# Attention with beacon keys and a maxout FFN on one core: batch 0's products by whole parts, a load gate one pair later, FFN two units ahead, no bank reordering

## The chip, the core and the metric

The kernel runs on one core of a Trainium2 chip. The metric is the device time of one execution in microseconds (us). TensorE (PE) multiplies matrices into PSUM (eight banks of 512 float32 columns on 128 partitions); VectorE (DVE), ScalarE (ACT) and GpSimd (POOL) do the rest; SyncE (SP) and GpSimd issue the transfers. Each engine works through its own instructions in the order in which they are written; semaphores hold an instruction until what it needs is there.

## The reference, cut to what matters

B = 8 batches, H = 8 heads, S = 576 tokens of D = 64, Nb = 16 beacon keys ahead of the tokens, d_model = 512, d_ff = 768.

```python
k_all, v_all = [beacon_k, k], [beacon_v, v]        # 592 keys
scores = q @ k_all.T / 8, causal over the 576 tokens, beacons always seen
a = exp(scores - max) / sum
x = (a @ v_all) as [4608 tokens, 512]
h = max(x @ w1, x @ w2, x @ w3)                    # [4608, 768]
out = h @ w_out                                    # float32
```

## The kernel before, in words

**Attention.** Heads go in pairs: pair p is two heads of batch p // 4, and two pairs make a quad (half of a batch). Scores are made transposed, keys on the partitions in five tiles t = 0..4 (128 keys each, the last 80), queries on the free axis; because of the mask, tile t needs only queries from 112, 240, 368 and 496 on. `emit_burst` (line 532) makes the scores of a pair (line 521, 12 matmuls) in four groups; each group takes a pair of PSUM banks, so a burst goes through all eight, in the order that `next_pairs` gives: bank pairs that were used longest ago first. ScalarE takes the exponential of each group (L541, L515 in batch 0), GpSimd (in batch 0 VectorE) masks it. `emit_pv_whole` (line 656) then makes a quad's sums over the keys (a product with ones, part 0) and its value products (parts 1 and 2: the even and the odd channels of four heads), line 684. ScalarE copies the products out (L694, L695) and inverts the sums by logarithm and exponential; `finish` (line 708) multiplies the two on VectorE into xT (L711), the transposed activations in a ring of four batches. The FFN of a block reads xT.

**Batch 0** is written by hand in `first_batch` (line 937), with scores of single pairs between other work, and with `pv_rest` (line 610) for the products of queries from 64 on: EARLY spans end at query 288 (HALF), LATE spans go from there to 576. P(quad, parts, early tiles, late tiles) emits some of them, line 592. `multiply_rest` (L648) multiplies products straight out of PSUM into xT; `invert_rest` makes the inverse sums on ScalarE (L633, L634). Early and late columns of one part lie in one bank.

**FFN.** It is cut into units, 22 for each block of 512 tokens: 18 first products (line 733; for each of six slices of d_ff the three weights i = 0, 1, 2), then four output products (line 786). i = 0 is copied into hT (L752), i = 1 and 2 are joined by a maximum on VectorE (L750); outputs are copied to y (L793) and stored by SP. In the first block the units are ordered and halved otherwise (line 763). A matmul of 512 columns takes a slot of 0.22 us, a first product four slots, an output product six. Units need xT of all their tokens. From pair 8 on, `emit_all` (line 1092) emits for each pair: the burst, every second pair the products of the quad before, then as many units as `allowed` admits (line 1107), then `finish`. The last unit of each step is the closing one: it is cut into 352 and 160 columns (CLOSE) in the two banks of the pair that `last_pair` gives, and drained in two halves. For a copy, ScalarE takes the 352 and VectorE the 160; for a maximum, VectorE takes both. The first unit is followed by the next pair's transposes (L405, up to pair 15), the second by the planned casts and loads. After pair 31 come its products, four units, `finish` and the rest of the units.

**Loads.** Batches 0 and 1 of q and k come through GpSimd's queue, cast on the way (`load_cast`, line 253), as do the FFN weights (`load_w`, L343; `load_w_out`, L346). The rest come through SP into seven staging buffers (L226, L305) and GpSimd casts them (L276, L321). The first of these for batch 2 are held back by a small memset on GpSimd (the gate, L224), emitted in `second_batch` (line 1046) among pair 6's masks. In that function pairs 4 to 7 run with three units each; `late_banks` moves two banks of quad 2's products to the end of the list of free banks, ahead of pair 8's burst.

Of the kernel before, what the change touches and what calls it, by code (L numbers as in the profile page):

```python
# [17 lines left out]
def kernel(  # L18
# [13 lines left out]
    nc = tc.nc  # L32

    B, H, S, D = q.shape
# [16 lines left out]
    HALF = S // 2  # L51


    n_kt = (NK + 127) // 128
# [3 lines left out]
    q_min = [max(0, t0) for t0 in k_tok]  # L58
# [545 lines left out]
            out = bank[:, part * HEAD : (part + 1) * HEAD]  # L604
            pv_matmuls(quad, part, out, 0, 0, HEAD, True, True)

    EARLY = [(0, HEAD, HALF), (1, q_min[1], HALF), (2, q_min[2], HALF)]
    LATE = [(t, max(HALF, q_min[t]), S) for t in range(n_kt)]

    def pv_rest(quad, parts, early, late=()):  # L610
        for part in parts:
            bank = pv_tiles[quad][part]
            for spans, ts in ((EARLY, early), (LATE, late)):
                for t in ts:
                    _, q0, q1 = spans[t]
                    pv_matmuls(
                        quad,
                        part,
                        bank[:, q0 - HEAD : q1 - HEAD],
                        t,  # L620
                        q0,
                        q1,
                        t == 0,
                        t == len(spans) - 1,
                    )

    def invert_heads(quad):
        nc.vector.reciprocal(recips[quad][:, 0:HEAD], pv_tiles[quad][3][:, 0:HEAD])
# [22 lines left out]
            recips[quad][:, None, q0:q1].to_broadcast([128, i1 - i0, q1 - q0]),  # L651
        )

    late_banks = []

    def emit_pv_whole(quad, order=(0, 1, 2, 3), split=False):
        b, g = divmod(quad, n_quad)
        v_sb = v_tiles[b]
        for p in range(PPQ * quad, PPQ * (quad + 1)):
            assert all((p, gi) in masked for gi in range(NG))  # L660
        banks = [next_bank() for _ in range(4)]
        banks = [banks[i] for i in order]
        late_banks[:] = [banks[0], banks[3]]
        every = range(n_kt)
        early = every[: V_PIECES[1][0]] if split else every
        runs = [(0, banks[0], 0, HEAD, S, every)]
        runs += [(part, banks[part], 0, HEAD, S, early) for part in (1, 2)]
        runs += [(part, banks[3], part * HEAD, 0, HEAD, every) for part in range(3)]
        if split:
            runs += [(part, banks[part], 0, HEAD, S, every[len(early) :]) for part in (1, 2)]  # L670
        for part, bank, lo, qa, qb, some in runs:
            ts = [t for t in every if q_min[t] < qb]
            for t in ts:
                if t not in some:
                    continue
                q0 = max(qa, q_min[t])
                n = k_rows[t]
                for j in range(4):
                    lhsT = (
                        ones[0:n]  # L680
                        if part == 0
                        else v_sb[0:n, t, head(g, j), part - 1 : D : 2]
                    )
                    nc.tensor.matmul(  # L684
                        acc[32 * j : 32 * j + 32, bank, lo + q0 - qa : lo + qb - qa],
                        lhsT,
                        at_view(PPQ * quad + j // 2, t, j % 2, q0, qb),
                        start=(t == 0),
                        stop=(t == ts[-1]),
                        tile_position=(0, 32 * j),  # L690
                    )
        raw = pv_pool.tile([128, 2, S], FP32, name="raw")
        for part in (1, 2):
            nc.scalar.copy(raw[:, part - 1, HEAD:S], acc[:, banks[part]])  # L694
        nc.scalar.copy(  # L695
            raw[:, :, 0:HEAD],
            acc[:, banks[3], HEAD : 3 * HEAD].rearrange("p (i c) -> p i c", i=2),
        )
        recip = nrm_pool.tile([128, S], FP32, name="recip")
        nc.scalar.activation(out=recip[:, HEAD:S], in_=acc[:, banks[0]], func=AF.Ln)  # L700
        nc.scalar.activation(out=recip[:, 0:HEAD], in_=acc[:, banks[3], 0:HEAD], func=AF.Ln)
        exp = partial(nc.scalar.activation, out=recip, in_=recip, func=AF.Exp, scale=-1.0)
        if split:
            between_exps.append(exp)
        else:
            exp()

        def finish():
            c0 = b % RING * S
            for i in range(2):  # L710
                nc.vector.tensor_mul(xT[:, 2 * g + i, c0 : c0 + S], raw[:, i], recip)  # L711
            if g == n_quad - 1:
                ready[0] = 2 * b + 1

        return finish
# [164 lines left out]
    def next_load(n=1, **gate):  # L880
        for _ in range(n):
            if loads:
                loads.pop(0)(**gate)
# [53 lines left out]
    def first_batch():  # L937
        T(2, 0, 0, 6, by_act)
        T(3, 0, 0, 7)
        load_v(0, 0, nc.vector)  # L940
        load_v(0, 1)
        load_beacons(1, B_PE, bk32_1)
        S_(1, 0)
        T(2, 0, 1, 5)
        T(3, 0, 1, 4)
        S_(2, 0)
        T(0, 1, 0, 6)
        T(0, 1, 1, 7)
        S_(3, 0)
        T(1, 1, 0, 5)  # L950
        T(1, 1, 1, 4)
        M(0, 0, True)
        S_(0, 1)
        fill(6)
        S_(0, 2)
        T(2, 1, 0, 6)
        T(3, 1, 0, 4)
        M(1, 0, True)
        S_(1, 1)
        T(2, 1, 1, 7)  # L960
        T(3, 1, 1, 5)
        S_(1, 2)
        S_(0, 3)
        for p in range(PPB):
            M(p, 1)
        M(0, 2, True)
        M(1, 2, True)
        V(0)
        load_w(0, [0])
        V(1)  # L970
        load_w(0, [1])
        V(2)
        load_cast(PPB)
        load_w(1, [0])
        V(3)
        load_w(1, [1])
        V(4)
        load_cast(PPB + 1)
        load_cast(PPB + 2)
        load_w(2)  # L980
        load_cast(PPB + 3)
        open_pv(0, acc[:, 4], acc[:, 5:7], acc[:, 7])
        P(0, (0,), (0, 1, 2))
        pv_heads(0)
        S_(1, 3)
        M(0, 3, True)
        M(1, 3, True)
        S_(2, 1)
        P(0, (0,), (), (0, 1, 3))
        S_(2, 2)  # L990
        M(2, 0, True)
        M(3, 0, True)
        P(0, (0,), (), (2, 4))
        S_(3, 1)
        M(2, 2, True)
        invert_heads(0)
        multiply_heads(0)
        P(0, (1, 2), (0, 1))
        S_(3, 2)
        S_(2, 3)  # L1000
        M(3, 2, True)
        P(0, (1, 2), (2,), (0, 1))
        S_(3, 3)
        M(2, 3, True)
        M(3, 3, True)
        P(0, (1, 2), (), (2,))
        first = sc_psum.tile()
        open_pv(1, first[:, 0], sc_psum.tile(), first[:, 1])
        P(1, (0,), (0, 1, 2))
        pv_heads(1)  # L1010
        P(1, (0,), (), (0, 1, 3))
        P(1, (0,), (), (2, 4))
        P(1, (1, 2), (0, 1, 2))
        for quad in range(n_quad):
            invert_rest(quad, HEAD, HALF)
        invert_heads(1)
        multiply_rest(0, HEAD, HALF)
        multiply_heads(1)
        for i in range(2):
            multiply_rest(1, HEAD, HALF, i, i + 1)  # L1020
        P(1, (1, 2), (), (0, 1, 2))
        for quad in range(n_quad):
            P(quad, (1, 2), (), (3,))
        for quad in range(n_quad):
            P(quad, (1, 2), (), (4,))
        ready[0] = 0
        for quad in range(n_quad):
            invert_rest(quad, HALF, S)
            multiply_rest(quad, HALF, S)
        by_act(bk16_1, bk32_1)  # L1030
        ready[0] = 1
        F_in(7, by_act)
        F_in(3, by_dve)
        F_in(4, by_act)
        turn_beacons(1, B_PE, bk16_1)
        place_beacons(PPB, by_act)
        F_in(5, by_dve)
        F_in(6, by_act)
        free_banks[:] = [0, 1, 2, 7, 3, 4, 5, 6]
        turn_pair(PPB, by_act)  # L1040
        load_v(1, 0, nc.vector)
        load_v(1, 1)
        drain[0] = by_dve
        F(1, last_pair(), True)

    def second_batch():
        for p in range(PPB, 2 * PPB):
# [6 lines left out]
            for gi in range(NG):  # L1054
                emit_masks(p, gi)
                if p == PPB + 2 and gi == 1:
                    cast_v(1, 0, by_pool)
            if p == PPB + 2:
                next_load(gate=nc.gpsimd)
                next_load(4)  # L1060
                cast_v(1, 1, by_pool)
            if p + 1 < 2 * PPB:
                F(1, next_psum)
# [5 lines left out]
        finish = emit_pv_whole(n_quad, (2, 0, 1, 3), True)  # L1069
        F(1, next_psum)  # L1070
        F(1, last_pair(), True)
        for i in late_banks:
            free_banks.remove(i)
            free_banks.append(i)
        return finish

    for p in range(B_PE * PPB, NPAIR):
# [14 lines left out]
    def emit_all():  # L1092
# [6 lines left out]
        for p in range(2 * PPB, NPAIR):  # L1099
# [4 lines left out]
            finish = emit_pv_whole(p // 2 - 1) if p % 2 == 0 else None  # L1104
            for gi in range(NG):
                emit_masks(p, gi)
            allowed = max((b - 1) * UPB + (-2, 4, 10, 16)[pi], done[0] + 2)
            n = 0
            while may_emit(allowed):
                n_y = len(y_out)  # L1110
# [60 lines left out]
```

## Time and profile before

| | |
|---|---|
| median of three runs | 284.36 us (284.12 to 284.95) |
| the profiled execution's own time | 284.03 us |
| its span, first to last instruction | 282.2 us |
| granted TensorE clock | 0.999 |
| busy: PE, DVE, ACT, POOL | 271.6, 171.1, 162.8, 133.0 us |
| mean busy share of the DMA engines until 230 us | about 0.9 and over |
| moved by DMA | 48.82 MB |

Times in the views count from the first instruction. A line of a timeline gives start, length, engine, line of the kernel, operation, what is written and read, the shape of the first of the merged instructions, how many, and in brackets the idle time ahead and what ended it. TensorE's lengths include the way through the array, so that neighbours overlap; starts are exact, and differences of starts are what the text uses. A few matmuls are missing from the counts. "issue" is time in which an engine waited for nothing that the profile shows.

### The profile page before, as it was taken

The page shows a single profiled execution, that of the slowest core. Times are in us where ns is not written, and L with a number is a line of the kernel's source. Part 1 is how long each engine was busy: PE and PEld are TensorE (multiplying, and loading weights), DVE is VectorE, ACT ScalarE, POOL GpSimd, SP SyncE. Part 2 cuts the span into 40 slices and gives each one's busy share as a digit, 9 for nine tenths or more (in the row PEclk, how much of TensorE's full clock was granted, in tenths as well). Part 3 has the DMA queues.
Part 4 walks back from the last instruction along what each step waited for, and adds up shares of the span by engine and source line. Part 5 has one row for each costly group of instructions (what it writes and reads, how often), then busy time and mean ns, then how long its engine had stood idle before and what let it go on. Part 6 is the DMA issues. An engine that isn't in the chain of part 4 may idle for free.

```text
span 282.2 us, 7689 instructions
## 1 busy us (share of the span) xinstructions
PE 271.6 (96%) x3020; PEld 156.4 (55%) x3050; DVE 171.1 (61%) x307; ACT 162.8 (58%) x307; POOL 133.0 (47%) x273
## 2 busy tenths in 40 slices
PE   7788999999999999999999999999999999999994
PEld 3557765556555555555556886555555554444442
DVE  4885655574837566464737382638363847876872
ACT  4995797978668566756675758585857540000000
POOL 7194378557286946475557655683245300000000
PEclk9999999999999999999999999999999999999999
DMA  8999989989997999999999999979745003003004
GB/s 145 214 180 204 219 159 159 241 200 293 275 205 229 199 241 245 186 249 207 250 194 189 252 243 242 187 161 236 184 105 172 0 2 149 2 1 149 0 0 149
DMA packets 85315, 48.82 MB, mean 173 GB/s; under 512 B 64416, under 2 KB 80032, under 8 KB 85280
## 3 DMA queue, kind: packets, MB, share of 16 engines
q1 hardware_dynamic: 78320, 42.25, 66.7%
q0 software_dynamic: 6544, 5.80, 13.5%
q8 instruction: 23, 0.38, 0.6%
q10 hardware_dynamic: 416, 0.30, 0.4%
q14 instruction: 12, 0.10, 0.1%
HBM read 35.13 MB, written 14.22 MB: 175 GB/s over the span
## 4 chain that ended last, share of the span: by engine, by line
PE 92%; ACT 4%; DVE 2%; issue 1%; DVEq 0%
PE acc L733 46%; PE acc L786 16%; PE acc L684 11%; PE acc L521 8%; PE acc L763 4%; ACT at_sb L515 4%; PE acc L405 2%; PE acc L465 1%; PE acc L592 1%; PE acc L804 0%; PE acc L506 0%; PE acc L424 0%; DVE kT L432 0%; DVE hT L750 0%; DVE busy L184 0%
## 5 line engine op out<-in xcount | busy, mean ns | idle before, releaser
L733 PE MATMUL acc<-xT,w_sb 128*128 128x512 bf16 (+4 forms) x728 | 134.2, 335 | 1.5 <-issue 0.2
L750 DVE TENSOR_TENSOR hT<-hT,acc 128x512 bf16<-128x512 bf16 (+1 forms) x104 | 70.2, 677 | 62.5 <-PE acc L733 55.2
L733 PEld LDWEIGHTS <-w_sb 128*128 128x128 bf16 x752 | 69.8, 98 | 59.5
L565 POOL TENSOR_SCALAR_AFFINE_SELECT at_sb<-at_sb 128x256 bf16<-128x256 bf16 x168 | 61.1, 385 | 81.5 <-ACT at_sb L541 80.8
L541 ACT ACTIVATE at_sb<-acc 128x208 bf16<-128x208 f32 (+3 forms) x140 | 89.6, 735 | 5.2 <-PE acc L521 3.3
L786 PE MATMUL acc<-w_out_sb,hT 128*128 128x512 bf16 (+2 forms) x241 | 48.3, 348 | 0.3
L752 ACT CAST hT<-acc 128x352 bf16<-128x352 f32 x18 | 8.1, 452 | 46.9 <-PE acc L733 46.9
L276 POOL CAST p<-st 96x768 bf16<-96x768 f32 x44 | 35.0, 824 | 0.0
L786 PEld LDWEIGHTS <-hT 128*128 128x128 bf16 x246 | 22.6, 98 | 22.0 <-DVE hT L750 1.9
L793 DVE COPY y<-acc 128x512 f32<-128x512 f32 (+1 forms) x35 | 22.0, 629 | 20.8 <-PE acc L786 15.2
L752 DVE CAST hT<-acc 128x512 bf16<-128x512 f32 (+1 forms) x48 | 26.6, 554 | 9.6 <-PE acc L733 9.1
L811 ACT COPY y<-acc 128x320 f32<-128x320 f32 x1 | 0.4, 426 | 46.0 <-PE acc L804 46.0
L521 PE MATMUL acc<-qT,kT 64*128 64x208 bf16 (+1 forms) x336 | 26.3, 279 | 0.2 <-DVE hT L750 0.2
L684 PE MATMUL acc<-at_sb,v_sb 128*32 128x336 bf16 (+5 forms) x672 | 22.8, 281 | 0.0
L521 PEld LDWEIGHTS <-kT 64*128 64x128 bf16 x336 | 15.4, 94 | 11.5 <-issue 1.1
L711 DVE TENSOR_TENSOR xT<-raw,recip 128x576 bf16<-128x576 f32 x28 | 20.7, 781 | 0.9 <-ACT recip L548 0.9
L321 POOL CAST v_sb<-st 128x1536 bf16<-128x1536 f32 (+2 forms) x21 | 18.3, 897 | 0.0
L684 PEld LDWEIGHTS <-v_sb 128*32 128x32 bf16 (+1 forms) x672 | 14.4, 97 | 6.6
L694 ACT COPY raw<-acc 128x512 f32<-128x512 f32 x28 | 15.7, 633 | 2.8 <-PE acc L684 2.8
L684 PE MATMUL acc<-at_sb,ones 128*32 128x512 bf16 (+3 forms) x336 | 14.9, 284 | 0.0
L515 ACT ACTIVATE at_sb<-acc 128x1024 bf16<-128x1024 f32 (+3 forms) x16 | 12.6, 864 | 0.8 <-PE acc L506 0.8
L763 PE MATMUL acc<-xT,w_sb 128*128 128x256 bf16 x96 | 11.7, 273 | 0.0
(76 smaller groups left out, 174.5 us busy)
## 6 DMA issues: line engine op xcount, KB each, us to landing
out_dram<-y SPq DMA_DIRECT2D x35, 256.0 KB, 3.4
st<-in_q_dram SPq DMA_DIRECT2D x22, 288.0 KB, 4.6
st<-in_k_dram SPq DMA_DIRECT2D x22, 288.0 KB, 5.1
st<-in_v_dram SPq DMA_DIRECT2D x24, 256.0 KB, 5.8
w_sb<-in_moe_w_dram POOLq DMA_DIRECT2D x6, 384.0 KB, 8.6
q_dram<-p SPq DMA_DIRECT2D x16, 144.0 KB, 2.5
k_dram<-p SPq DMA_DIRECT2D x16, 144.0 KB, 2.4
st<-in_v_dram SPq DMA_DIRECT2D x8, 224.0 KB, 6.1
```

The lines of the kernel that those rows point to most:

```text
L276: cast(t16.rearrange("p r h d -> p h r d"), st[0:QP, i * NQ2 : (i + 1) * NQ2].rearrange("p (h r d) -> p h r d", h=2, r=QR),)
L515: nc.scalar.activation(out=both_heads(p, gi), in_=ps[:, :, 0 : g_width(p, gi)], func=AF.Exp, scale=scale)
L521: nc.tensor.matmul(ps, kTs[p % NT][hs, 128 * t : 128 * t + 128], qTs[p % NT][hs, q0:q1], start=True, stop=True, tile_position=(64 * e, 0),)
L541: nc.scalar.activation(out=both_heads(p, gi)[:, e0:e1], in_=acc[:, first + e0 : first + e1, 0 : g_width(p, gi)], func=AF.Exp, scale=scale,)
L565: nc.gpsimd.affine_select(out=view, in_=view, compare_op=ALU.is_ge, fill=0.0, base=x0, pattern=[[0, 2], [1, hi - lo]], channel_multiplier=-1,)
L684: nc.tensor.matmul(acc[32 * j : 32 * j + 32, bank, lo + q0 - qa : lo + qb - qa], lhsT, at_view(PPQ * quad + j // 2, t, j % 2, q0, qb), sta ...
L733: nc.tensor.matmul(ps[:, a:b], w_in[i][:, ct, 128 * ft : 128 * (ft + 1)], xT[:, ct, x0 : x0 + b - a], start=(ct == 0), stop=(ct == n_ct - 1),)
L750: nc.vector.tensor_max(h[:, lo:hi], h[:, lo:hi], ps[:, lo:hi])
L752: (by_act if hi < TOKB else by_dve)(h[:, lo:hi], ps[:, lo:hi])
L763: nc.tensor.matmul(ps, w_in[i][:, ct, 128 * (ft + f) : 128 * (ft + f + 1)], xT[:, ct, tb * TOKB + lo : tb * TOKB + hi], start=(ct == 0), s ...
L786: nc.tensor.matmul(ps[:, lo:hi], hT[:, ft, 128 * tt : 128 * (tt + 1)], w_out_sb[:, ft, lo:hi], start=(ft == 0), stop=(ft == n_ft - 1),)
L793: (by_act if hi < d_model else by_dve)(y[:, lo:hi], ps[:, lo:hi])
```

## The change

- Batch 0: tile 0's product of queries 64 to 576 is one matmul of 512 columns instead of one of 224 (EARLY) and one of 288 (LATE). Quad 0's parts 1 and 2 get their remaining tiles earlier, and quad 1's parts 1 and 2 are each completed ahead of the multiplication of their first half.
- Second batch: the gate and the five load requests behind it move from the end of pair 6's masks to behind the second mask group of pair 7, behind the cast of batch 1's values.
- `allowed` rises by two in every step from pair 8 on.
- The reordering of two banks ahead of pair 8 goes.

```diff
-    EARLY = [(0, HEAD, HALF), (1, q_min[1], HALF), (2, q_min[2], HALF)]
-    LATE = [(t, max(HALF, q_min[t]), S) for t in range(n_kt)]
+    EARLY = {0: (HEAD, S), 1: (q_min[1], HALF), 2: (q_min[2], HALF)}
+    LATE = {t: (max(HALF, q_min[t]), S) for t in range(1, n_kt)}
...
-        P(0, (0,), (), (0, 1, 3))
+        P(0, (0,), (), (1, 3))
...
-        P(0, (1, 2), (2,), (0, 1))
+        P(0, (1, 2), (2,), (1,))
...
-        P(0, (1, 2), (), (2,))
+        P(0, (1, 2), (), (2, 3))
         first = sc_psum.tile()
         open_pv(1, first[:, 0], sc_psum.tile(), first[:, 1])
         P(1, (0,), (0, 1, 2))
         pv_heads(1)
-        P(1, (0,), (), (0, 1, 3))
+        P(1, (0,), (), (1, 3))
+        P(0, (1, 2), (), (4,))
         P(1, (0,), (), (2, 4))
-        P(1, (1, 2), (0, 1, 2))
         for quad in range(n_quad):
             invert_rest(quad, HEAD, HALF)
         invert_heads(1)
         multiply_rest(0, HEAD, HALF)
         multiply_heads(1)
-        for i in range(2):
-            multiply_rest(1, HEAD, HALF, i, i + 1)
-        P(1, (1, 2), (), (0, 1, 2))
-        for quad in range(n_quad):
-            P(quad, (1, 2), (), (3,))
-        for quad in range(n_quad):
-            P(quad, (1, 2), (), (4,))
+        for part in (1, 2):
+            P(1, (part,), (0, 1, 2), (1, 2, 3, 4))
+            multiply_rest(1, HEAD, HALF, part - 1, part)
...
+                if p == PPB + 3 and gi == 1:
+                    next_load(gate=nc.gpsimd)
+                    next_load(4)
             if p == PPB + 2:
-                next_load(gate=nc.gpsimd)
-                next_load(4)
                 cast_v(1, 1, by_pool)
...
-        for i in late_banks:
-            free_banks.remove(i)
-            free_banks.append(i)
...
-            allowed = max((b - 1) * UPB + (-2, 4, 10, 16)[pi], done[0] + 2)
+            allowed = max((b - 1) * UPB + (0, 6, 12, 18)[pi], done[0] + 2)
```

More of the change, by code (lines that the diff above doesn't have):

```diff
@@ L614, in pv_rest @@
                 for t in ts:
[L615 to L625, printed above, removed]
+                    q0, q1 = spans[t]
+                    out = bank[:, q0 - HEAD : q1 - HEAD]
+                    pv_matmuls(quad, part, out, t, q0, q1, t == 0, t == n_kt - 1)
     def invert_heads(quad):
@@ L652, in multiply_rest @@
         )
-    late_banks = []
     def emit_pv_whole(quad, order=(0, 1, 2, 3), split=False):
@@ L662, in emit_pv_whole @@
         banks = [banks[i] for i in order]
-        late_banks[:] = [banks[0], banks[3]]
         every = range(n_kt)
```

## The prediction

> **What bounds the kernel now.** I read the head of the page first, then the chain of work that ended last, then the list of TensorE's waits, and then timelines of the places that the change touches.
>
> ```profile
> PE 92%; ACT 4%; DVE 2%; issue 1%; DVEq 0%
> ```
>
> ```profile
> PE acc L465 <- DVE busy L184: 1.5, 1, 1.5
> PE acc L506 <- ACT at_sb L515: 1.1, 3, 0.6
> PE acc L592 <- DVE xT L648: 0.9, 1, 0.9
> ```
>
> The chain is TensorE at 92%. The lines of the second fence give, for an engine and a line, who was waited for, us in total, times and the longest; TensorE's eight such lines sum to 4.9 us, all but 0.4 of it before 24 us. From there on TensorE runs its fixed order without holes. So a wait that goes is worth its length, and a wait that is added costs its length: no later hole takes it up. The largest wait that the change can touch is the 0.9 at line 592.
>
> **Batch 0, products by whole parts.** Columns first: nothing is dropped. A 224-column and a 288-column product become one of 512, in six groups of four. Successive groups start at streaming rate (1,728 columns from 21.90 to 22.65, 2.3 columns per ns), so 24 fewer instructions are worth under 0.1 us. [...]
>
> The gain is in the order. The timeline of 20 to 24 us:
>
> ```profile
> 20.40 0.60 PE L592 MATMUL acc<-at_sb,v_sb 128*32 128x224 bf16 x24
> 21.90 1.01 PE L592 MATMUL acc<-at_sb,v_sb 128*32 128x288 bf16 x27 [0.90 <-DVE xT L648]
> 23.16 0.66 PE L592 MATMUL acc<-at_sb,v_sb 128*32 128x208 bf16 x29 [0.26 <-issue]
> 23.76 0.50 PE L763 MATMUL acc<-xT,w_sb 128*128 128x256 bf16 x3
> ```
>
> The late columns of quad 1 go into banks whose early columns VectorE is still multiplying, so TensorE waits. In the changed order each part is complete before its multiplication, and quad 0's remaining products are done earlier, where TensorE waited for the last exponentials and masks. Left at 20.40 are two parts of 1,600 columns, 1.39 us at the rate above. I add 0.15, because two longer products (2 x 288 columns, 0.24 us) now stand ahead of the scores of pair 3 at 17.14 and ScalarE, busy without a break until 20, gets these late. The products end at 21.94.
>
> Then two things decide when FFN starts. The last multiplication (0.34 us, half of the 0.69 for two; about 0.2 after its product, as at 23.86) ends at 22.5, and the fourth FFN matmul needs it, 0.33 us in: an effective start of 22.23. The third matmul needs the second half of the first FFN weight; GpSimd's queue waited 1.05 us for a w_sb transfer until 22.41 (in the instruction order that queue entry and the third matmul wait for the same counter), so it is there by then, which fits the same start. Gain 23.76 - 22.23 = 1.53. The hold from 22.65 to 23.16 has no cause in the trace; if it comes back, the gain is 1.03. I take **-1.4**.
>
> **No bank reordering.** Scores of pair 8 used the bank pair of the closing FFN unit second; now they use it last, as pairs 5 to 7 do. Pair 8's scores took 1.41 us (50.07 to 51.48), pair 7's 1.00 (43.30 to 44.30), with the same kind of unit ahead: **-0.41**.
>
> **FFN two units ahead.** The limit moves from 20 to 22 at pair 8, so this step issues four output units (L786) instead of two, and every later step the same number as before, shifted by two. The instruction order of the changed kernel confirms it. TensorE's work is the same; three covers go.
>
> (a) Before, the first pair of each batch ended with two of the four output units and the next pair began with the other two, while VectorE made xT. Now all four come first and the next pair begins with a unit that reads the new xT. VectorE's queue holds the closing copy and then both multiplications:
>
> ```profile
> 88.41 0.90 PE L521 MATMUL acc<-qT,kT 64*128 64x208 bf16 x12
> 88.57 0.33 DVE L793 COPY y<-acc 128x160 f32<-128x160 f32 x1 [0.67 <-ACT y L793]
> ...
> 88.81 1.62 DVE L711 TENSOR_TENSOR xT<-raw,recip 128x576 bf16<-128x576 f32 x2
> ...
> 89.24 1.47 PE L786 MATMUL acc<-w_out_sb,hT 128*128 128x512 bf16 x5
> ```
>
> Scores start at 88.41, the next unit 0.83 later, and its fourth matmul (0.216 apart) 1.48 after 88.41. It needs the second multiplication, which ends 2.02 after; with 0.05 for the semaphore that is 0.59 lost. At pairs 9 and 17 the same rows give 0.60 and 0.59; at 25 and 29 (1.42 for the two) 0.39 each; at 21, where the ring's end cuts the unit in two, 0.28. The first multiplication is just in time for the third matmul. Sum **+2.84**. Behind the waiting matmul stand the next pair's transposes and five units; they all slip.
>
> (b) The same at the end:
>
> ```profile
> 234.59 0.69 DVE L793 COPY y<-acc 128x512 f32<-128x512 f32 x1 [0.60 <-PE acc L786]
> 235.20 1.42 DVE L711 TENSOR_TENSOR xT<-raw,recip 128x576 bf16<-128x576 f32 x2
> ...
> 236.98 0.59 PE L733 MATMUL acc<-xT,w_sb 128*128 128x512 bf16 x2
> ```
>
> Two output units (2.6 us) run between the copy's product and 236.98. Now nothing does: four output units end 5.18 after 230.07, at 235.25; the copy runs from 235.45 (0.20 after, as now 234.59 after 234.39) and the multiplications follow 0.61 later, ready at 236.81 and 237.48; the third and fourth matmuls, due at 235.68 and then 0.22 after the third, wait 1.18 and 0.45: **+1.63**.
>
> (c) Each step's last unit is drained in two halves. Before, they were first products (i = 0) or output units: ScalarE takes 352 columns, VectorE 160, side by side. Shifted by two, all but the four-unit steps close with i = 2, a maximum, both halves on VectorE. The scores' last group goes into these banks. Pair 7 has just that ahead of it, pair 11 the old closing:
>
> ```profile
> 73.53 0.45 ACT L752 CAST hT<-acc 128x352 bf16<-128x352 f32 x1 [2.09 <-PE acc L733]
> ...
> 73.70 0.91 PE L521 MATMUL acc<-qT,kT 64*128 64x208 bf16 x12
> 73.87 0.32 DVE L752 CAST hT<-acc 128x160 bf16<-128x160 f32 x1 [0.26 <-PE acc L733]
> ...
> 74.55 0.39 PE L733 MATMUL acc<-xT,w_sb 128*128 128x512 bf16 x1
> ```
>
> Scores took 0.85 there and 1.00 at pair 7: 0.154 each. Seventeen bursts follow such a step (pairs 10 to 31 without 13, 17, 21, 25, 29): **+2.62**.
>
> **Loads at pair 7's masks.** The gate goes behind one cast and two masks on GpSimd, from 45.58 to about 47.4, less the 1.4 gained. Behind it on SP stand ten loads and the first stores. Pair 10's cast ran at 55.12, after masks, not waiting for data (landing 4.6 to 5.1 in the median). Step 8 is now two output units (2.6 us) longer, and in the later four-unit steps the store of the first output stands ahead of loads on SP, up to 3 us later than now, but no GpSimd wait for data after 24 us exceeds 0.6. Cost 0, hidden by the masks of pair 8 and by loads that run several casts ahead; without that cover some 0.4. On the other side, pair 9's cast loads, the slowest of their kind (13.1 us at most, the last issued at 41.7), get the queues alone for longer. Bounds 0 and +1.5 (below).
>
> **Sum.** 284.03 (the profiled execution's own time; span 282.2) - 1.4 - 0.41 + 2.84 + 1.63 + 2.62 = 289.3. That execution lies 0.33 under the median of 284.36, so I give **289.5**.
>
> **Rivals.**
> 1. The closing halves cost nothing (c = 0), since TensorE's group and VectorE's last maximum could fall differently once (a) has delayed things: 286.9. For it: the third group's margin was only 0.04 us before, so small shifts matter. Against: pairs 7 and 8 both show it. 11%.
> 2. Data late: pair 9's k lands at 54.8 (41.7 + 13.1) whatever happens, and TensorE transposes it at 55.14 - 1.8 = 53.3: +1.5, and the hold at 22.65 stays: +0.4, so 291.4. Against: GpSimd issues it 1.4 earlier and the gate spares it competitors. 11%.
> 3. Faster: VectorE's closing work is no longer behind TensorE. (a), (b) and (c) share one place, VectorE's queue at a step's end. If its copy and multiplications ended 0.6 us sooner (and 1.6 at the tail), all three vanish: 282.2. It decides at 1.48 us after the scores' start. The rows say 1.82 to 2.03 at each of five places, and the order of the queue is unchanged. 2%; in between, at no change, 2%.
> 4. The clock. [...] 1%.
>
> That the FFN is not ahead at all is ruled out by the instruction order. My forecast has the remaining 73%.
>
> **Range.** 286.9 to 291.2: down to rival 1, up to most of rival 2. About 0.3% is what a measurement of this kernel can tell from no change; faster 2%, same 2%, slower 96%.
>
> **What would show it.** FFN starts near 22.2 and L648's wait is gone; pair 8's scores take 1.0; TensorE's waits list a new FFN wait on xT, some twelve to fourteen times, 4.5 us in all, and scores waiting for hT, some 2.6 over 17 bursts; the CAST of 352 columns on ScalarE is gone after pair 8. Wrong if the first unit after pairs 9, 13, 17 starts its fourth matmul within 1.6 us of the scores' start, or if scores stay at 0.85.

## The result and the profile after

| | before | after |
|---|---|---|
| median (range, executions) | 284.38 us (284.01 to 286.41, 6) | 294.95 us (293.80 to 295.99, 6) |
| ratio, 95% interval | | 1.0357 [1.0317, 1.0396] |
| the profiled execution's own time, span | 284.03, 282.2 | 294.04, 292.3 |
| first FFN matmul | 23.76 | 24.40 |
| pair 4's scores start | 30.15 | 31.00 |
| from there to the last matmul | 248.21 | 257.45 |

The change costs 3.6%: 10.6 us between the medians, 10.0 between the profiled executions; the prediction said 5 (289.5). Executions of one kernel differ by up to 5 us, while in the traces of one schedule the interval from pair 4's scores to the last matmul repeats to 0.02 us, so I compare that interval (the last row) beside the whole.

The head of the chain and the waits list of the changed kernel (engine, line, who was waited for: us in total, times, longest):

```profile
PE 86%; DVE 5%; ACT 4%; issue 2%; DMA 1%; POOL 1%; POOLq 0%; ACTq 0%
```

```profile
PE acc L722 <- DVE xT L700: 3.0, 7, 1.0
PE acc L592 <- issue: 1.6, 1, 1.6
PE acc L506 <- ACT at_sb L515: 1.6, 4, 0.6
```

(Line numbers after 600 are 8 to 11 lower than before.) The first wait is the one the prediction added; line 592's wait on VectorE is gone as forecast, but a longer one has come in its place that is put down to nothing ("issue"; 0.3 before). TensorE's timeline at the end of batch 0:

```profile
21.03 1.53 PE L592 MATMUL acc<-at_sb,v_sb 128*32 128x512 bf16 x51
24.18 0.29 PE L592 MATMUL acc<-at_sb,v_sb 128*32 128x208 bf16 x5 [1.62 <-issue]
24.40 0.82 PE L752 MATMUL acc<-xT,w_sb 128*128 128x256 bf16 x4
```

The products run through without a wait, and then TensorE stands still (last start 22.31, next 24.18) ahead of the last five tiny products, the first of them 0.22 before FFN.

The waits of FFN on xT are there too. In pair 13's step the fourth matmul was due at 94.40 (three slots of 0.216 after 93.75) and starts at 95.00:

```profile
93.75 0.82 PE L722 MATMUL acc<-xT,w_sb 128*128 128x512 bf16 x2
95.00 0.38 PE L722 MATMUL acc<-xT,w_sb 128*128 128x512 bf16 x1 [0.42 <-DVE xT L700]
```

The waits list does not show the largest item. From the first matmul of a pair's scores to the first matmul after them takes 1.13 to 1.21 at the seventeen pairs that follow a closing unit with i = 2, 1.18 in the mean; before, the same seventeen took 0.86, and the prediction said 1.00. Pair 11, whose rows of before stand in the prediction (73.70 to 74.55):

```profile
76.74 1.20 PE L521 MATMUL acc<-qT,kT 64*128 64x208 bf16 x12
77.86 1.04 PE L722 MATMUL acc<-xT,w_sb 128*128 128x512 bf16 x3
```

TensorE counts as busy there, because matmuls overlap; only differences of starts show it.

### The profile page after: what moved, and what is told of

It is laid out like the page before. It is cut to its first block, busy times and chain, and to the rows that moved or that the text cites. A ratio compares the mean times of both kernels' runs of the same rounds, so it can differ in the third digit from the quotient of the medians.

```text
span 292.3 us, 7616 instructions
## 1 busy us (share of the span) xinstructions
PE 277.9 (95%) x2996; PEld 156.7 (54%) x3026; DVE 179.8 (61%) x325; ACT 154.9 (53%) x289; POOL 133.7 (46%) x273
## 4 chain that ended last, share of the span: by engine, by line
PE 86%; DVE 5%; ACT 4%; issue 2%; DMA 1%; POOL 1%; POOLq 0%; ACTq 0%
PE acc L722 43%; PE acc L775 13%; PE acc L673 10%; PE acc L521 8%; PE acc L752 4%; DVE xT L700 3%; ACT at_sb L515 2%; PE acc L405 2%; PE acc L592 2%; PE acc L465 1%; DMA st<-in_q_dram 1%; DVE y L782 1%; PE acc L506 1%; ACT y L782 1%; ACT at_sb L541 1%
## 5 line engine op out<-in xcount | busy, mean ns | idle before, releaser
L565 POOL TENSOR_SCALAR_AFFINE_SELECT at_sb<-at_sb 128x256 bf16<-128x256 bf16 x168 | 61.9, 390 | 91.0 <-ACT at_sb L541 86.6
L739 DVE TENSOR_TENSOR hT<-hT,acc 128x512 bf16<-128x512 bf16 (+2 forms) x122 | 71.3, 599 | 20.7 <-PE acc L722 14.2
L741 DVE CAST hT<-acc 128x512 bf16<-128x512 f32 x48 | 33.2, 691 | 30.2 <-PE acc L722 16.9
L775 PE MATMUL acc<-w_out_sb,hT 128*128 128x512 bf16 (+2 forms) x237 | 46.8, 347 | 0.5
L521 PE MATMUL acc<-qT,kT 64*128 64x208 bf16 (+1 forms) x336 | 31.7, 280 | 0.0
L700 DVE TENSOR_TENSOR xT<-raw,recip 128x576 bf16<-128x576 f32 x28 | 21.7, 818 | 0.9 <-ACT recip L548 0.9
L782 ACT COPY y<-acc 128x352 f32<-128x352 f32 x6 | 2.7, 453 | 13.8 <-PE acc L775 13.8
```

The source lines that it names most:

```text
L521: nc.tensor.matmul(ps, kTs[p % NT][hs, 128 * t : 128 * t + 128], qTs[p % NT][hs, q0:q1], start=True, stop=True, tile_position=(64 * e, 0),)
L565: nc.gpsimd.affine_select(out=view, in_=view, compare_op=ALU.is_ge, fill=0.0, base=x0, pattern=[[0, 2], [1, hi - lo]], channel_multiplier=-1,)
L739: nc.vector.tensor_max(h[:, lo:hi], h[:, lo:hi], ps[:, lo:hi])
L741: (by_act if hi < TOKB else by_dve)(h[:, lo:hi], ps[:, lo:hi])
L775: nc.tensor.matmul(ps[:, lo:hi], hT[:, ft, 128 * tt : 128 * (tt + 1)], w_out_sb[:, ft, lo:hi], start=(ft == 0), stop=(ft == n_ft - 1),)
L782: (by_act if hi < d_model else by_dve)(y[:, lo:hi], ps[:, lo:hi])
```

## The experiments

In all of them the last row of the table above, "from pair 4's scores to the end", is called the rest.

### Batch 0: what TensorE waits for ahead of FFN

TensorE's records can be counted. Ahead of the hold the trace of before has 352 weight loads and 350 matmuls, one for one on every line but two, where one matmul each is missing; so I count the loads and take each as two records, the load and its matmul. In the trace of before the unexplained hold (22.65 to 23.16) lies behind the 352nd load, which is record 704; in the changed kernel, whose order there is another, the stop lies behind record 704 as well. Among the transfers there is a queue of kind "instruction" that brings 23 blocks of 16,384 bytes within the span. From the start of one of its transfers to that of the next TensorE passes 253 such records in the mean in either trace (22 intervals, 108 to 466 each), and 256 in before with a 24th block that starts 1.0 behind the last instruction. The block whose transfer ended at 21.90 before and 22.87 after was followed by TensorE's restart 1.27 and 1.32 later. So my theory became: TensorE runs out of instructions. Its rival: data, a weight or VectorE, unseen.

**ffn_old.** The changed kernel with the old limit:

```diff
-            allowed = max((b - 1) * UPB + (0, 6, 12, 18)[pi], done[0] + 2)
+            allowed = max((b - 1) * UPB + (-2, 4, 10, 16)[pi], done[0] + 2)
```

> The changed kernel with the limit of FFN units as before (20 at pair 8); batch 0 by whole parts, the gate at pair 7 and the missing bank reordering stay. Theory (instruction supply): TensorE may not start its instruction 705 before a fetched block of 256 instructions has arrived; in both traces it stops exactly ahead of number 705 (22.65 to 23.16 before, 22.30 to 24.17 after). So FFN starts at about 24.2 (23.8 to 24.5) with TensorE stopped ahead of the same number; pair 8's scores take 1.0; scores after pair 8 take 0.85. Time 284.4 + 0.7 - 0.4 = 284.7. Rival 1 (my prediction's terms): FFN starts at 22.2, time 284.4 - 1.4 - 0.4 = 282.6. Rival 2 (the moved gate starves a later cast): a GpSimd wait for data over 0.6 and a TensorE wait behind it, 285.5 or more.

Measured: ratio 0.9987 [0.9950, 1.0023], median 284.49 against 284.60. The stop is there again behind record 704 (24.32 to 25.25; this execution had a granted clock of 0.50 from 12 to 20 us, so the whole start is later). The rest is 247.92, 0.29 less than before. So the whole loss of the change comes with the FFN limit, and the other parts together are worth nothing that this measurement can tell. GpSimd's waits for transfers after 26 us are 1.6 for one cast load of batch 1 (on a weight's counter) and 0.6 here and there, and no TensorE wait stands behind them: rival 2 is out. One surprise: scores of pair 8 take 1.00, but pair 9 starts no earlier. TensorE now waits 0.39 more for a bank ahead of the closing unit of step 8; with four output units in that step this wait is covered. The 0.29 are other small waits that moved with the bank order (0.08 at pair 15, 0.21 at pair 24).

**after_pad32.** The changed kernel with tiny matmuls ahead of everything:

```diff
+    def pad(n):
+        ps = pv_bank(1)
+        for i in range(n):
+            j = 32 * (i % 4)
+            nc.tensor.matmul(
+                ps[j : j + 32, 0:16], busy[:, 0:32], busy[:, 0:16], start=True, stop=True, tile_position=(0, j)
+            )
...
-        keep_busy(8, 480)
+        keep_busy(7, 480)
+        pad(17)
```

> The changed kernel with 17 tiny matmuls in place of one warm-up matmul: 32 instructions more. Instruction supply: TensorE stops ahead of number 705 again, which is now 16 products earlier (20 of quad 1's last products stand behind the stop, not 4), and since number 449 is passed about 0.6 earlier the stop ends about 0.6 earlier, near 23.6; FFN starts near 24.0; time 0.4 less, 294.5. Rival (a wait for data): the stop stays ahead of the last four products and its length stays.

```profile
20.74 1.18 PE L592 MATMUL acc<-at_sb,v_sb 128*32 128x512 bf16 x35
22.93 0.64 PE L592 MATMUL acc<-at_sb,v_sb 128*32 128x176 bf16 x21 [1.01 <-issue]
23.49 0.93 PE L752 MATMUL acc<-xT,w_sb 128*128 128x256 bf16 x5
```

The stop kept its number (704) and moved sixteen products back: 35 ahead of it and 21 behind, in place of 51 and 5. A wait for data would have kept its product. It ended at 22.92, 1.26 earlier than in the changed kernel (I had expected 0.6, an estimate from the time at which record 449 is passed; no run shows that the stop depends on that record), since the block's transfer also started earlier (20.62). Four executions (295.40, ratio 1.0325 [1.0264, 1.0385]) can't resolve so small a gain in the whole time.

**ffn_old_pad112 and ffn_old_pad112_b.** `ffn_old` with `keep_busy(6, 480)` and `pad(58)` (112 records more), twice.

> The same with 58 tiny extra matmuls (16 columns, results not used) in place of two of the eight warm-up matmuls at the start: 112 instructions more ahead of batch 0. [...] The stop of 1 to 2 us ahead of FFN goes (0.3 at most stays, at another instruction), FFN starts at 22.4 (22.2 to 22.8), time 1.6 to 2.0 under the run without the extra matmuls: 282.9. Rival (TensorE waits for data, weights or VectorE that the trace doesn't show): the stop stays ahead of the same product, FFN at 24.2, time equal.

> The same kernel as ffn_old_pad112 once more, on another set of executions, since the first set spread over 4 us. If the stop is gone for good, the undisturbed executions lie 1.1 to 1.3 under the undisturbed ones of the kernel before (282.7 against 283.9), and the profile shows no stop over 0.3 at line 592. If the padding brings a new stop in some executions (a later block of instructions that comes late), the spread of this kernel stays wider than that of the kernel before, with times 3 to 4 higher at full clock.

Second set, TensorE's timeline:

```profile
21.00 1.59 PE L592 MATMUL acc<-at_sb,v_sb 128*32 128x512 bf16 x56
22.52 1.70 PE L752 MATMUL acc<-xT,w_sb 128*128 128x256 bf16 x12
```

All 56 products in one piece, FFN at 22.72 and 22.52, no stop. The block's transfer started at 15.77 and 16.49, in place of 21.93. Times: first set 285.17 with a range of 282.65 to 287.03 (ratio 0.9983 [0.9943, 1.0023], undecided), second set 282.78, ratio 0.9932 [0.9899, 0.9965]. In the first set five of twelve executions with a clock of 0.998 or more took 284.8 to 287.0; a possible reason comes below.

**before_pad112.** The kernel before with the same padding alone.

> The kernel before with the 58 tiny matmuls alone. Instruction supply: no stop at instruction 705, but the wait of 0.9 for VectorE at line 592 (21.9) stays, so the products run through and FFN starts at 23.25 (the 0.51 of the stop), 283.5 to 283.9 in undisturbed runs, between the kernel before (283.9) and the changed batch 0 with the same padding (282.7). If FFN starts at 22.7 here too, the order of the products was worth nothing. If it stays at 23.76, the stop of the kernel before had another cause.

```profile
21.28 0.60 PE L592 MATMUL acc<-at_sb,v_sb 128*32 128x224 bf16 x24
22.78 1.42 PE L592 MATMUL acc<-at_sb,v_sb 128*32 128x288 bf16 x56 [0.90 <-DVE xT L648]
24.14 1.05 PE L763 MATMUL acc<-xT,w_sb 128*128 128x256 bf16 x8
```

The stop is gone here too: 1.36 from the restart to FFN, 1.86 before. FFN's absolute start, 24.14, missed my 23.25, since this execution's last exponential ended 0.88 later (20.80 for 19.92). The padded kernels also give what the order of the products is worth when instructions are there: from the end of batch 0's last exponential to FFN it takes 3.33 in the old order and 2.00 in the new. Of this gain 0.21 is lost again behind FFN's start: in the new order its fourth matmul waits for the last multiplication, and pair 4's scores come 6.60 after FFN's start instead of 6.39. Time 287.70, ratio 1.0030 [0.9986, 1.0073]: seven of twelve executions took 287.7 to 288.1, so two more executions were profiled.

**before_pad112_b, before_pad112_c.** The same kernel, one execution each.

> The kernel before with the 58 tiny matmuls, one more look: 7 of its 12 executions took 287.7 at full clock, 3.9 above the rest. If this look falls among them (about even odds), its trace shows where: a stop of TensorE ahead of instruction 449, 705 or 961 if it is the instruction supply again, otherwise a wait for a transfer, with the name of the tile in the waits list.

> As before_pad112_b, a second look for the executions of 287.7.

Both fell among the long ones (286.94 and 287.21). TensorE's timeline near the start, first of before_pad112, then of before_pad112_c:

```profile
6.05 0.40 PE L506 MATMUL acc<-qT,kT 64*128 64x48 bf16 x6
...
6.87 0.45 PE L424 MATMUL acc<-ident,quad 96*64 96x96 bf16 x12
```

```profile
6.48 0.61 PE L506 MATMUL acc<-qT,kT 64*128 64x48 bf16 x6
...
7.62 0.69 PE L424 MATMUL acc<-ident,quad 96*64 96x96 bf16 x12
```

The same six score matmuls took 0.61 in place of 0.40, twelve transposes 0.69 in place of 0.45, and so on until about 20.9 (in before_pad112_b until about 17.5), with a granted clock of 1.00 in the rows. These are the lengths of the records themselves, not waits for instructions or for a transfer, and no view shows what made them longer. I had cut two of the eight 480-column matmuls of `keep_busy` (the warm-up matmuls of the expectations), which may be the reason. In before_pad112_b the block's transfer started only at 21.53, and the stop behind record 704 was back (22.95 to 23.81). In before_pad112_c it started at 20.14, and there was no stop, although record 449 (256 ahead of the stop) was passed at 17.2 in both: the time of that record alone does not set when the block comes.

**ffn_old_pad116_warm.** `ffn_old` with `pad(58)` and all eight warm-up matmuls.

> The changed kernel with the old limit of FFN units and the 58 tiny matmuls, all eight warm-up matmuls kept (they were six in the earlier padded kernels). The two looks at the padded kernel before that took 287 showed TensorE at half its rate until past 15 us (six score matmuls 0.61 instead of 0.40) with a granted clock of 1.00. Theory (two warm-up matmuls fewer leave TensorE slow in some executions): the times gather at 282.5 to 283.2 with at most the share of high ones that the kernel before has (about a third over 285). Rival (the padding itself or the chip brings the slow ones): 3 or more of 12 lie 3 us higher at full clock. No stop ahead of instruction 705, FFN starts by 22.9. Against the kernel before: 0.4 to 0.6 per cent faster.

Measured: 283.23 (282.60 to 286.01) against 285.21, ratio 0.9941 [0.9911, 0.9972]. Nine of twelve lie at 282.6 to 283.5; the three above have a granted clock of 0.986 to 0.988; none is 3 us higher at full clock. FFN starts at 22.82 without a stop. With ffn_old_pad112_b (the first set of that kernel was undecided) this is the version that beats both kernels: batch 0 by whole parts, the FFN limit of before, and padding.

### The FFN limit: which unit closes a step

**before_ffn2.** The kernel before with `(0, 6, 12, 18)` alone.

> The kernel before with one part of the change alone: the limit of FFN units two higher from pair 8 on. The accounts of the changed kernel's trace give for it: late multiplications after the four-output steps 2.3, their longer closing 0.3, the tail 1.6, closing halves 5.5, so 284.4 + 9.7 = 294.1; the scores ahead of which such a closing stands take 1.13 to 1.21. My prediction's terms gave 2.84 + 1.63 + 2.62, so 291.5, with scores of 1.00. If a good part of the loss needs the other edits (the moved gate, the bank order), the time is under 292.5 while the scores take over 1.1.

Measured: 294.26, ratio 1.0297 [1.0244, 1.0350]; rest 257.86, 9.65 more than before. The seventeen scores take 1.18 in the mean, as in the changed kernel, and the rest is 0.41 longer than there, which is pair 8's scores (1.41). The limit alone makes the loss.

**after_slice_pairs.** The order of the first products in blocks 1 to 8:

```diff
-            for ft in range(n_ft):
-                for i in range(3):
-                    units.append((need, mm1_unit, (tb, ft, i)))
+            for ft in range(0, n_ft, 2):
+                for i in range(3):
+                    for f in range(2):
+                        units.append((need, mm1_unit, (tb, ft + f, i)))
```

> The changed kernel with the first products of blocks 1 to 8 ordered by pairs of slices (i = 0 for two slices, then i = 1, then i = 2). The closing unit is still a maximum with i = 2, both halves on VectorE, but the unit ahead of it belongs to another slice. Theory (VectorE waits for its own previous result): the closing maximum no longer reads what the maximum right before it writes, so it starts without the 0.1 us gap, and scores after these steps take 1.00, as at pair 7, instead of 1.13 to 1.21: 17 x 0.17 = 2.9 less, 292.0. Rival (VectorE is simply later in these steps, or ScalarE's exponential sets the end): scores stay at 1.13 to 1.21, time 295.

VectorE's timeline ahead of pair 10's scores, first in the changed kernel, then here (a 512-column maximum and the two closing halves, merged):

```profile
66.78 1.55 DVE L739 TENSOR_TENSOR hT<-hT,acc 128x512 bf16<-128x512 bf16 x3 [0.23 <-PE acc L722]
```

```profile
67.30 1.35 DVE L739 TENSOR_TENSOR hT<-hT,acc 128x512 bf16<-128x512 bf16 x3 [0.23 <-PE acc L722]
```

The same three instructions take 0.20 less. In the changed kernel the 352-column half starts 0.10 after the end of the 512-column maximum, whose result it reads (same slice, i = 1 and i = 2); at pair 7 of before, where consecutive maxima are of different slices, it starts 0.02 ahead of that end, and the three take 1.42. With slices in pairs the scores take 0.99 in the mean (pair 23's stay at 1.20); the rest falls by 3.21, and the sum of the seventeen by 20.07 - 16.86 = 3.21. The whole: 290.68, ratio 1.0168 [1.0100, 1.0236], 4.3 under the changed kernel's 294.95, of which 3.2 are explained by the rest; the other 1.1 is not explained, and executions scatter by as much.

**after_plus3.** `(1, 7, 13, 19)`: FFN three units ahead, so that a copy (i = 0) or an output closes.

> The changed kernel with the limit three instead of two units above the old one (1, 7, 13, 19). One unit further ahead, but the closing units are i = 0 (a copy, ScalarE and VectorE side by side) or outputs again; the first unit after a four-output (here three- or four-output) step still needs the new xT. Theory (the loss sits in which unit closes, not in how far FFN is ahead): scores take 0.85 again everywhere, 5.5 less, time 289.4; the waits on xT stay at 0.5 each and 1.6 in the tail. Rival (FFN ahead costs by itself): 295 or more.

Measured: 291.33, ratio 1.0209 [1.0146, 1.0273]; rest 253.41, 4.04 less than the changed kernel. The scores take 0.84 in the mean again, 5.73 less in sum, so it is the closing unit and not the distance. But my 5.5 did not arrive: something new costs 1.5. Step 11, TensorE, VectorE and TensorE's weight loads:

```profile
82.96 1.74 PE L775 MATMUL acc<-w_out_sb,hT 128*128 128x352 bf16 x12
83.22 0.69 DVE L739 TENSOR_TENSOR hT<-hT,acc 128x512 bf16<-128x512 bf16 x1 [0.23 <-PE acc L722]
83.96 0.54 PEld L775 LDWEIGHTS <-hT 128*128 128x128 bf16 x7 [0.45 <-DVE hT L739]
```

The closing unit is now the block's first output, right behind the last maximum, and its sixth matmul loads the slice that this maximum is still writing: 0.41 between two starts that are 0.15 apart otherwise, in each of the steps 11, 15, 19, 23, 27 and 31. Six times 0.26 is 1.5.

**after_finish_early.** The multiplications into xT are emitted after the first output unit, in the steps with four of them and in the tail:

```diff
             while may_emit(allowed):
+                if finish and pi == 0 and n == 1:
+                    finish()
+                    finish = None
...
-        for _ in range(4):
+        emit_ffn(END, next_psum)
+        finish()
+        for _ in range(3):
             emit_ffn(END, next_psum)
-        finish()
```

> The changed kernel with the two multiplications into xT placed after the first of the four output units, in steps 8, 12, 16 to 28 and in the tail, instead of behind the closing one. Theory: TensorE's waits for xT (3.0 in the waits list, 4.2 by the starts) come only from VectorE's order, so they go: 2.3 + 0.3 + 1.6 less, 290.8, or 291.5 if the output copies that now stand behind the multiplications hold up a bank. The closing halves keep scores at 1.13 to 1.21. Rival (the multiplications are held by ScalarE's inverse sums or by PSUM, not by VectorE's order): the waits stay, 294 to 295.

Line 722's wait on xT (3.0) is gone from the list. What is left of such waits:

```profile
PE acc L521 <- DVE y L782: 0.2, 1, 0.2
```

Rest 253.60, 3.85 less; whole 291.74, ratio 1.0190 [1.0138, 1.0242]. By the starts, steps 9, 17, 21, 25 and 29 gain 0.61, 0.60, 0.28, 0.39 and 0.39, the tail 1.63. Step 13 gains nothing: there the multiplications took 2.61 and the output copies behind them held a bank that pair 13's scores wanted (1.43 for 0.83).

## Why the prediction was wrong in size

By its own terms, for the profiled execution (it forecast +5.3 against 284.03; measured +10.0):

| step | predicted | measured | from |
|---|---|---|---|
| batch 0 | -1.4 | +0.85 | pair 4's scores, 30.15 to 31.00 |
| pair 8's scores | -0.41 | -0.41 | 1.41 to 1.00 |
| (a) xT after four outputs | +2.84 | +2.79 | six waits by the starts in the changed kernel |
| (b) tail | +1.63 | +1.63 | the same (1.18 and 0.45); after_finish_early |
| (c) closing halves | +2.62 | +5.51 | seventeen scores, 14.56 to 20.07 |
| loads | 0 | 0 | GpSimd's waits, ffn_old's rest |
| other small waits | - | -0.28 | remainder of the last interval's 9.24 |

The terms make 10.1, which is the difference of the spans. The last row is what the others leave. It is not the bank order: before_ffn2 has the old one and the same remainder (9.65 less 2.78, 1.63 and 5.52). Most of it is one wait of 0.2 in the kernel before, ahead of pair 25's scores (from pair 24 to 25 it took 7.76, from 20 to 21 and from 28 to 29 7.53), which neither the changed kernel nor ffn_old has.

**Batch 0** is the step with the wrong sign. "Left at 20.40 are two parts of 1,600 columns" and "The products end at 21.94" were right in kind: the wait on VectorE went, and by the padded kernels the reordering is worth 3.33 - 2.00 = 1.33 up to FFN and, with the 0.21 that FFN's fourth matmul waits as forecast, 1.12 up to pair 4's scores. The prediction had 1.03 with the hold left as it was, or 1.18 without the 0.15 that it took off for late exponentials; executions scatter too much ahead of the last exponential to tell those 0.15.

What failed is the sentence "The hold from 22.65 to 23.16 has no cause in the trace; if it comes back, the gain is 1.03". It had a cause that the trace does hold: TensorE does not pass record 704 before a block of instructions is there (in nine traces it went on 1.2 to 1.5 after that transfer's end). Removing the wait ahead of it lets TensorE arrive earlier at the same closed door, and removing 24 matmuls (48 records) only brings the door 48 records closer to FFN. The stop was 1.87 instead of 0.51, so it took the whole 1.33 back, and FFN stood 3.86 behind the last exponential where it had stood 3.84.

What is left of the +0.85 is that 0.21 and a last exponential that ended 0.63 later (20.55 for 19.92). Of that, 0.43 is already there at the first exponential (6.91 for 6.48), ahead of every changed instruction: two 320-column warm-up matmuls behind the first transposes took 0.73 in this execution and 0.44 in that of before. This part is the luck of two executions, not the change.

Shown: the stop keeps its record number through nine traces with four different orders ahead of it, moves by sixteen products when 32 records are added, and goes when the block comes early enough (in five padded traces). Not shown: what sets when the block comes. Its transfer starts 2.6 to 4.3 us behind record 449, from which the expectation of after_pad32 counts, in the traces with a stop and 1.0 to 3.2 in those without; neither that record nor the load on the transfer queues was tested as the cause.

**(c)** is the term that was mis-sized, 0.154 each by the step "Pair 7 has just that ahead of it". Pair 7 is not the same: in block 0 units are ordered by i, so two maxima in a row belong to different slices. In the later blocks the closing maximum reads what the maximum before it wrote, on the same engine. That is worth 0.19 each (3.21 over seventeen): after_slice_pairs takes just this away and leaves 0.135 each (16.86 - 14.56 over seventeen), which is what the prediction meant by its 0.154.

**(a), (b) and pair 8** were right, (b) to the hundredth, and for the forecast reason: in the changed kernel the matmul that needs the new xT, behind the scores of pairs 9, 13, 17, 21, 25 and 29, is late by 0.59, 0.59, 0.59, 0.26, 0.38 and 0.38, and the tail's two waits are 1.18 and 0.45, 4.4 in all where the waits list shows 3.0. after_finish_early takes them away, but at pair 13 its own new wait costs as much. That pair 8's 0.41 arrives at all depends on the longer step behind it: with the old limit it is lost again at once. Of the rivals, "The closing halves cost nothing" fell; the granted clock read 1.00 in the profile after; the late data did not come.

## What to carry to other kernels

A hold for which the profile names no releaser is to be counted before it is written off: if it lies at the same instruction number of its engine in two kernels, the instruction supply is the first suspect, a few instructions of padding can test it, and reordering work ahead of it gains nothing here until the block comes earlier. A row that is taken as a model for a cost has to match in its dependencies too, above all in whether an instruction reads what the one before it on the same engine wrote. Where a schedule runs with no slack, shifting it by a unit or two changes which unit stands at every boundary; here that cost more (5.5) than either wait on xT.

## What the runs showed of the hardware

- TensorE stopped behind its 704th record in nine traces, for 0.5 to 2.1 us, and restarted 1.2 to 1.5 us after the recorded end of a 16,384-byte instruction transfer. In the changed kernel 51 of the narrow products, 102 records with their loads, start within 1.28 us (21.03 to 22.31); at that rate the 253 records that came per transfer would pass in 3.2 us, an estimate from these numbers.
- 58 matmuls of 16 columns that compute nothing, with the changed batch 0, bring the kernel 0.6% under the kernel before (0.9941 [0.9911, 0.9972]): the stop is gone, and FFN starts at 22.82 (24.40 in the changed kernel). The changed batch 0 alone is 0.9987 [0.9950, 1.0023].
- With six in place of eight warm-up matmuls of 480 columns TensorE's records were 1.5 times as long until about 17.5 and 20.9 us in the two traces before_pad112_b and before_pad112_c, while the granted clock read 1.00; by their times, so they were in seven of twelve executions of before_pad112. That the missing two are the cause is supported by ffn_old_pad116_warm, which had none of these, but not shown: of two sets of one kernel with six, ffn_old_pad112 had up to five in twelve and ffn_old_pad112_b at most one, and the kernel before, with eight, has single executions of 287.6 and 288.9 at a clock of 1.00. Six and the padding fill 3.1 us ahead of the first transposes (1.53 to 4.60 in before_pad112_c), eight fill 3.4 in the kernel before (1.54 to 4.90); what makes the records longer is not shown.
- A VectorE maximum that reads the result of the one before it starts 0.10 after that one's end; without such a dependency it starts 0.02 (pair 7 of before) to 0.08 (after_slice_pairs) ahead of the end.
